# A second Strassen level for one of the seven gate/up block products

## The chip, the cores and the metric

One core of one Trainium2 chip. The metric is the time of one execution on the device, in microseconds (us), as the median of several runs; the run with a profile is one of them, except for the kernel before, whose profiled run (739.01 us) is a separate one. Most runs agree within 0.3%, which is half of what this change can move at most, so the experiments were timed in five rounds against the kernel before on the same chip.

## The reference, cut to what matters

```python
h  = x + attention(layernorm(x))                  # S = 2048 tokens, D = 1024, linear attention, 32 heads
def _B_ref(x, W_gate, W_up, W_down):              # x: (1, 2048, 1024), F = 3584
    gate = jnp.einsum("bsd,df->bsf", x, W_gate)
    up   = jnp.einsum("bsd,df->bsf", x, W_up)
    gate = gate * (gate > 0)
    h = gate * up
    return jnp.einsum("bsf,fd->bsd", h, W_down)
h2 = h + _B_ref(layernorm(h), W_gate, W_up, W_down)
```

All inputs are bf16. The change touches only the two products `gate` and `up`.

Of the kernel before, what the change touches and what calls it, by code (L numbers as in the profile page):

```python
# [8 lines left out]
ALU = mybir.AluOpType  # L9
FP32 = mybir.dt.float32  # L10
BF16 = mybir.dt.bfloat16
# [20 lines left out]
def block_kernel(ctx: ExitStack, tc: tile.TileContext, x, wqkv, wo, wg, wu, wd, out, H: int):  # L32
# [449 lines left out]
    def new_hn(s):  # L482
        aops = mctx.enter_context(tc.tile_pool(name=f"aops{s}", reuse_waits="tile", bufs=1))
        hnT.append([aops.tile([P, KC, SW], BF16, name=f"hn{s}{i}") for i in range(2)])
        hns.append([aops.tile([P, KH, SW], FP16, name=f"hs{s}{k}") for k in range(3)])
# [136 lines left out]
    qctx.close()  # L622


    new_hn(1)
    tpool = mctx.enter_context(tc.tile_pool(name="tpool", reuse_waits="tile", bufs=2))
    mwork = mctx.enter_context(tc.tile_pool(name="mwork", reuse_waits="tile", bufs=2))
# [28 lines left out]
            out.append(ops())  # L656
        return out

    H22, S1, S2, S3, H12, S4, H21 = range(7)

    def wd_sums(c):

        st = {}
        tt = nc.vector.tensor_tensor

        def load():
            raw = fpool.tile([P, 4 * D], BF16, tag="wraw", bufs=2, name="wraw")[:].rearrange("p (k c d) -> p k c d", k=2, c=2)
            for k in range(2):
                nc.sync.dma_start(out=raw[:, k], in_=wd_k[:, k, 2 * c:2 * c + 2, :])
            st["b"] = [[raw[:, k, :, j * DW:(j + 1) * DW] for j in range(2)] for k in range(2)]  # L670

        def one():
            t = fpool.tile([P, 4 * D], BF16, tag="wt", name="wt")
            st["t"] = t[:].bitcast(FP16).rearrange("p (k c d) -> p k c d", k=4, c=2)
            (b11, b12), _ = st["b"]
            tt(out=st["t"][:, 0], in0=b12, in1=b11, op=ALU.subtract)

        def two():
            tt(out=st["t"][:, 1], in0=st["b"][1][1], in1=st["t"][:, 0], op=ALU.subtract)

        def three():
            tt(out=st["t"][:, 2], in0=st["b"][1][1], in1=st["b"][0][1], op=ALU.subtract)

        def four():
            tt(out=st["t"][:, 3], in0=st["b"][1][0], in1=st["t"][:, 1], op=ALU.subtract)
            for k in range(4):
                nc.sync.dma_start(out=t_dram[k][:, 2 * c:2 * c + 2, :], in_=st["t"][:, k])

        return load, [one, two, three, four]

# [15 lines left out]
        nc.sync.dma_start(out=x_dram[s][k][:, H12:S4 + 1, r, :], in_=hq[:, H12:S4 + 1, :])  # L706

    def new_hq():
        return spool[0].tile([P, 7, SW], BF16, tag="hq", bufs=3, name="hq")

    def early_sums(f):

        k, r = divmod(f, FQ)
        st = []

        def load():
            st.append(new_hq())
            nc.sync.dma_start(out=x1[0][k][:, r, :], in_=raw_dram[0][:, f, :])
            for q, j in ((3, H22), (2, H21), (1, H12)):
                nc.sync.dma_start(out=st[0][:, j, :], in_=raw_dram[q][:, f, :])  # L720

        return [load, lambda: None, lambda: None, lambda: hh_sums_a(st[0], 0, f), lambda: hh_sums_b(st[0], 0, f)]
# [3 lines left out]
    def early_quad(s, fc, w):  # L726

        left = left_ops(hnT[s], hns[s])
        gus = {}

        def mm(ps, m, v, start):
            for kc in range(KH):
                nc.tensor.matmul(ps[:], lhsT=w(v, m)[:, kc, :], rhs=left[m - 1][:, kc, :],  # L733
                                 start=(start and kc == 0), stop=(kc == KH - 1), skip_group_check=True)

        def fin(i, j, v, ps, m):
            q = 2 * i + j
            if v == 0:
                gus[q] = mwork.tile([P, 2, SW], BF16, tag="gu", name="gu")
            gu = gus[q]  # L740
            if m is not None:
                nc.vector.tensor_tensor(out=gu[:, v, :], in0=ps[:], in1=m, op=ALU.add)
            if v == 0:
                nc.scalar.activation(out=gu[:, 0, :], in_=ps[:] if m is None else gu[:, 0, :], func=ACT.Relu)
            else:
                d = mwork.tile([P, SW], BF16, tag="hh1", bufs=4, name="hh1")
                nc.vector.tensor_tensor(out=d[:], in0=gu[:, 0, :], in1=ps[:] if m is None else gu[:, 1, :], op=ALU.mult)
                nc.sync.dma_start(out=raw_dram[q][:, fc, :], in_=d[:])

        return strassen(pspool, mwork, mm, fin, 4, False, quad_copies[fc])  # L750
# [39 lines left out]
    for t, copy in ((order[-2], ("m1", 1)), (order[-1], ("u3", 1))):  # L790
        tc.add_manual_dep(squared[t].ins, quad_copies[2][copy].ins.name,
                          mybir.DependencyInfo(mybir.DependencyClass.NoSync, mybir.DependencyReason.DATA),
                          reason="order")
    pqctx.close()
    psctx.close()
    abctx.close()
# [2 lines left out]
    x1pool = ctx.enter_context(tc.tile_pool(name="x1pool", side="right", **reuse))  # L799
    fpool = ctx.enter_context(tc.tile_pool(name="fpool", side="right", **reuse))  # L800
    sctx = ExitStack()
    spool.append(sctx.enter_context(tc.tile_pool(name="spool", side="right", **reuse)))
    ET = mybir.EngineType
    ctx.enter_context(tc.manual_schedule(engines={ET.PE, ET.DVE, ET.Activation}))
# [7 lines left out]
    x1 += new_x(x1pool)  # L812
    add = nc.vector.tensor_tensor

    def quad(s, fc, w, k):

        left = left_ops(hnT[s], hns[s])
        tag = "XY"[k % 2]
        hq = new_hq()
        out = {0: x1[s][fc // FQ][:, fc % FQ, :], 1: hq[:, H12, :], 2: hq[:, H21, :], 3: hq[:, H22, :]}  # L820
        st = {}

        def halves(t):
            return t[:].rearrange("p (v n) -> p v n", v=2)

        def m(n, nm, t=None):
            if t:
# [5 lines left out]
                                     start=(t is not None and kc == 0), stop=(kc == KH - 1), skip_group_check=True)  # L833

        def snap(nm):
            st[nm] = mwork.tile([P, 2, SW], FP32, tag="snap", bufs=4, name="snap")
            nc.scalar.copy(out=st[nm][:], in_=halves(st["A"]))  # L837

        def gu(q, nm, base):
# [5 lines left out]
            add(out=out[q], in0=st[q][:, 0, :], in1=st[q][:, 1, :], op=ALU.mult)  # L845

        def rg():
            st["rg"] = mwork.tile([P, SW], BF16, tag="rg", name="rg")
            nc.scalar.activation(out=st["rg"][:], in_=halves(st["A"])[:, 0, :], func=ACT.Relu)

        def mul2():
# [2 lines left out]

        return {
            "m1": lambda: m(1, "A", "A"), "s1": lambda: snap("m1"), "m2": lambda: m(2, "D", tag),
            "g0": lambda: gu(0, "D", "m1"), "x0": lambda: mul(0), "m6": lambda: m(6, "A"), "s2": lambda: snap("u2"),
            "m5": lambda: m(5, "E", tag), "m7": lambda: m(7, "A"), "s3": lambda: snap("u3"),
            "g3": lambda: gu(3, "E", "u3"), "x3": lambda: mul(3), "m4": lambda: m(4, "A"), "rg": rg, "x2": mul2,
            "m3": lambda: m(3, "E"), "g1": lambda: gu(1, "E", "u2"), "x1": lambda: (mul(1), hh_sums_b(hq, s, fc)),  # L860
        }

    HW = DW // 2
# [59 lines left out]
    for steps, _ in now:  # L923
        for f in steps:
            f()
    prv, k = None, 0
    for r, (wt, f, fi, toks) in enumerate(runs):
        w = [ops() for _, ops in now]
        later = []
        for n, s in enumerate(toks):  # L930
            first = n == 0 and isinstance(wt, int) and fi == 0
            due = (wt + 1 if first else NE // GP if r == GP else 0)
            if r + 1 < len(runs) and n == 0 and not (r == NE - 1):
                now = sums_of_run(r + 1)
                later = [p for steps, _ in now for p in steps]
            take = -(-len(later) // (len(toks) - n))
            work += later[:take]
            del later[:take]
            if r >= NE:
                want = -(-len(fill) // max(nwin - 2 - k, 1))  # L940
                for p in range(want):
                    work.insert(min(len(work), 2 * p + 1), fill.pop(0))
            cur = quad(s, f, w, k)
            cur["m1"]()
            cur["s1"]()
            if prv:
                prv["g3"]()
                slot(0)
                prv["x3"]()
            cur["m2"]()  # L950
            if prv:
                prv["m4"]()
            cur["g0"]()
            slot(1)
            cur["x0"]()
            if prv:
                prv["rg"]()
            cur["m6"]()
            slot(2)
            if prv:  # L960
                prv["x2"]()
            cur["s2"]()
            if prv:
                prv["m3"]()
            if due and due < FH // GP:
                get_group(due)
            slot(3)
            if r == NE - 1:
                now = sums_of_run(r + 1)
                work += [p for steps, _ in now for p in steps]  # L970
            cur["m5"]()
            if prv:
                prv["g1"]()
                slot(4)
                prv["x1"]()
            cur["m7"]()
            cur["s3"]()
            slot(5)
            assert not work
            prv = cur  # L980
            k += 1
# [19 lines left out]
    for n in range(2):  # L1001
        t = fpool.tile([P, 4 * D], BF16, tag="wraw", bufs=2, name="xd")
        fview.append(t[:, 0:FQ * SW].rearrange("p (f t) -> p f t", f=FQ))
    ftile = fpool.tile([P, 4 * D], BF16, tag="wt", name="xd")
    xs_free = [ftile[:, 0:FQ * SW].rearrange("p (f t) -> p f t", f=FQ).bitcast(FP16)]
    for i, t in ((1, fview[0]), (0, fview[1])):
        xtiles[1, i, 0] = t
# [388 lines left out]
```

## The kernel before: what the change and the argument touch

Every large product is done as one level of Strassen in Winograd's form: the operands are cut in 2 x 2 blocks, and seven block products, with sums of blocks as operands, replace eight. In the gate/up stage the tokens and F are halved for the result's blocks, and D for the contraction. A "window" is the work for one tile of 128 columns of F, in both halves of F, and one half of the tokens, for gate and up together. `quad` holds its steps: `m1` to `m7` are the block products on TensorE, `s1` to `s3` copies of a running sum out of PSUM (ScalarE), `g0`, `g1`, `g3` joins of a second PSUM accumulator with such a copy (VectorE), each followed by a ReLU on ScalarE, and `x0` to `x3` the products of gate and up (VectorE).

```python
def quad(s, fc, w, k):
    left = left_ops(hnT[s], hns[s])
    tag = "XY"[k % 2]
    hq = new_hq()
    ...
    def m(n, nm, t=None):                      # one block product: 8 matmuls of 512 columns
        if t:
            st[nm] = acc(t)                    # a new accumulator: [128, 1024] fp32, gate and up
        ps = halves(st[nm])
        for v in range(2):
            for kc in range(KH):               # KH = 4 contraction tiles
                nc.tensor.matmul(ps[:, v, :], lhsT=w[v][n - 1][:, kc, :], rhs=left[n - 1][:, kc, :],
                                 start=(t is not None and kc == 0), stop=(kc == KH - 1), ...)

    def snap(nm):                              # ScalarE: PSUM -> fp32 in SBUF
        st[nm] = mwork.tile([P, 2, SW], FP32, tag="snap", bufs=4, name="snap")
        nc.scalar.copy(out=st[nm][:], in_=halves(st["A"]))

    def gu(q, nm, base):                       # VectorE: join PSUM with a copy; ScalarE: ReLU of the gate half
        g = st[q] = mwork.tile([P, 2, SW], BF16, tag="gu", name="gu")
        add(out=g[:], in0=halves(st[nm]), in1=st[base][:], op=ALU.add)
        nc.scalar.activation(out=g[:, 0, :], in_=g[:, 0, :], func=ACT.Relu)

    def mul(q):
        add(out=out[q], in0=st[q][:, 0, :], in1=st[q][:, 1, :], op=ALU.mult)
    ...
    return {
        "m1": lambda: m(1, "A", "A"), "s1": lambda: snap("m1"), "m2": lambda: m(2, "D", tag),
        "g0": lambda: gu(0, "D", "m1"), "x0": lambda: mul(0), "m6": lambda: m(6, "A"), "s2": lambda: snap("u2"),
        "m5": lambda: m(5, "E", tag), "m7": lambda: m(7, "A"), "s3": lambda: snap("u3"),
        "g3": lambda: gu(3, "E", "u3"), "x3": lambda: mul(3), "m4": lambda: m(4, "A"), "rg": rg, "x2": mul2,
        "m3": lambda: m(3, "E"), "g1": lambda: gu(1, "E", "u2"),
        "x1": lambda: (mul(1), hh_sums_b(hq, s, fc)),   # activation product, one more sum, a store
    }
```

The loop over windows writes the steps of this window and the tail of the previous one (`prv`) in one fixed order. In this stage TensorE, VectorE and ScalarE run exactly the order written. `slot(n)` puts in "filling" pieces of VectorE work: the sums of the next tile's weights, the sums of the down weights, and sums of the activations that an earlier stage stored.

```python
cur["m1"](); cur["s1"]()
prv["g3"](); slot(0); prv["x3"]()
cur["m2"](); prv["m4"]()
cur["g0"](); slot(1); cur["x0"]()
prv["rg"](); cur["m6"](); slot(2); prv["x2"](); cur["s2"]()
prv["m3"](); ...; slot(3)
cur["m5"](); prv["g1"](); slot(4); prv["x1"]()
cur["m7"](); cur["s3"](); slot(5)
```

The sums of the down weights work on 1024 columns at a time, from a load buffer `wraw` into a buffer `wt`, and are stored to DRAM for the down stage.

## Time and profile before

| | value |
|---|---|
| median (3 runs) | 738.68 us (738.03 to 740.35) |
| span of the profiled run | 737.2 us |
| gate/up stage | from 288 to 578 us, 24 windows of 12.09 us |
| TensorE in that stage | 56 matmuls a window, 0.2159 us start to start, no idle time |
| VectorE in that stage | 222 us busy, 77% |

The profile page's fourth part follows the chain of work that ended last back from the end, and gives its shares by engine. Of the kernel before:

```profile
PE 85%; DVE 7%; DMA 4%; ACT 3%; issue 1%; SPq 0%; DVEq 0%; POOL 0%; ACTq 0%
```

TensorE (PE) carries it. VectorE (DVE) has slack. In the list of waits of VectorE in the gate/up stage (columns: engine, what waited, what it waited for; us in total, times, longest) the top line is

```profile
DVE tg L640 <- PE accA L832: 21.9, 11, 2.0
```

The first weight sum for the next tile waits for a buffer of weight sums that TensorE is still reading: 11 times, about 2.0 us each. This is idle time of an engine off the path. It costs nothing here, but it shows that VectorE's 77% can't all be moved about at will.

### The profile page before, as it was taken

The numbers are of one execution on the slowest core, as the hardware profiler recorded it, in microseconds if no ns is written. First come the engines' busy times: TensorE is split into PE (matmuls) and PEld (weight loads), VectorE is DVE, ScalarE is ACT, GpSimd is POOL, SyncE is SP. The second block draws the span as 40 slices with busy tenths as digits, with TensorE's granted clock in tenths as the row PEclk, the third lists the DMA queues.
The fourth block names the chain that finished last, engine by engine and source line by source line (L and its number), as shares of the span: only waits on it lengthen the run. The fifth ranks groups of instructions, "written<-read, shape, count | busy, mean of one in ns | idle before, by whom it ended". The sixth has DMA issues, their size and how long they took to land.

```text
span 737.2 us, 10549 instructions
## 1 busy us (share of the span) xinstructions
PE 722.7 (98%) x3967; PEld 381.8 (52%) x4020; DVE 556.0 (75%) x980; ACT 321.5 (44%) x580; POOL 20.7 (3%) x56
## 2 busy tenths in 40 slices
PE   8999999999989999999999999999999999999997
PEld 3444555444444444444444444444444458888667
DVE  6997644676789767688768787887786479996677
ACT  4776553778786655444344444443444120000000
POOL 0000000000000000000000000000000001100210
PEclk9999999999999999999999999999999999999999
DMA  9765002079977526175638358575483499978932
GB/s 315 169 145 157 0 1 95 21 168 230 215 166 166 135 73 208 43 207 135 196 106 243 114 188 270 182 219 193 162 280 120 137 392 343 305 253 283 257 44 58
DMA packets 143811, 128.88 MB, mean 175 GB/s; under 512 B 50960, under 2 KB 126096, under 8 KB 143760
## 3 DMA queue, kind: packets, MB, share of 16 engines
q1 hardware_dynamic: 136688, 123.30, 55.6%
q0 software_dynamic: 5312, 3.15, 3.4%
q10 hardware_dynamic: 1760, 1.77, 0.7%
q8 instruction: 31, 0.51, 0.3%
q14 instruction: 20, 0.16, 0.1%
HBM read 76.81 MB, written 39.85 MB: 158 GB/s over the span
## 4 chain that ended last, share of the span: by engine, by line
PE 85%; DVE 7%; DMA 4%; ACT 3%; issue 1%; SPq 0%; DVEq 0%; POOL 0%; ACTq 0%
PE accA L832 22%; PE accX L832 8%; PE accY L832 8%; PE accA L1167 8%; PE attn L557 6%; PE Aq L733 4%; PE Aq L314 3%; PE accA L993 3%; PE accX L1167 3%; PE Aq L454 3%; PE accY L1167 2%; PE Eq L314 2%; PE accY L993 2%; PE accX L993 2%; PE Eq L733 2%; DVE stats L272 1%
## 5 line engine op out<-in xcount | busy, mean ns | idle before, releaser
L842 ACT ACTIVATE gu<-gu 128x512 bf16<-128x512 bf16 x72 | 45.4, 630 | 131.3 <-DVE gu L841 131.3
L837 ACT COPY snap<-accA 128x1024 f32<-128x1024 f32 x72 | 72.5, 1008 | 36.5 <-PE accA L832 36.4
L832 PEld LDWEIGHTS <-tg 128*128 128x128 f16 x384 | 37.6, 98 | 45.3
L832 PEld LDWEIGHTS <-tu 128*128 128x128 f16 x384 | 37.6, 98 | 45.3
L557 PE MATMUL attn<-wo_mem,oT 128*128 128x512 bf16 x247 | 57.9, 379 | 2.6 <-DVE o_sb L534 1.3
L841 DVE TENSOR_TENSOR gu<-accY,snap 128x1024 bf16<-128x1024 f32 x36 | 43.9, 1219 | 10.0 <-ACT snap L837 10.0
L832 PE MATMUL accA<-hn,tg 128*128 128x512 f16 (+1 forms) x192 | 49.3, 379 | 0.0
L832 PE MATMUL accA<-hn,tu 128*128 128x512 f16 (+1 forms) x192 | 49.3, 379 | 0.0
L841 DVE TENSOR_TENSOR gu<-accX,snap 128x1024 bf16<-128x1024 f32 x36 | 43.9, 1219 | 6.4 <-PE accX L832 3.7
L154 ACT COPY u<-Aq 128x512 f32<-128x512 f32 x54 | 31.3, 581 | 36.6 <-PE Aq L314 19.3
L1167 PEld LDWEIGHTS <-x 128*128 128x128 f16 (+1 forms) x448 | 43.9, 98 | 5.5
L832 PEld LDWEIGHTS <-wu 128*128 128x128 bf16 x288 | 28.2, 98 | 34.0
L832 PEld LDWEIGHTS <-wg 128*128 128x128 bf16 x288 | 28.2, 98 | 34.0
L557 PEld LDWEIGHTS <-oT 128*128 128x128 bf16 x256 | 24.6, 98 | 32.5 <-issue 4.1
L845 DVE TENSOR_TENSOR hq<-gu 128x512 bf16<-128x512 bf16 x48 | 20.3, 423 | 14.3 <-ACT gu L842 14.2
L314 PEld LDWEIGHTS <-xT 128*128 128x128 bf16 (+1 forms) x192 | 18.6, 98 | 23.6 <-issue 2.3
L534 DVE TENSOR_TENSOR o_sb<-nd,rd 128x384 bf16<-128x384 f32 (+1 forms) x48 | 23.4, 508 | 8.3 <-ACT rd L533 6.1
L1131 POOL DMA_DIRECT2D out_dram<-o x12 | 15.2, 1265 | 508.8 <-DMA h<-h_dram 419.1
L1167 PEld LDWEIGHTS <-xs 128*128 128x128 f16 x280 | 27.4, 98 | 3.2
L560 DVE SCALAR_TENSOR_TENSOR x_res<-attn,x_res 128x512 bf16<-128x512 f32 x32 | 22.0, 686 | 8.6 <-PE attn L557 8.5
L1173 DVE TENSOR_TENSOR snap<-accA,u 128x1024 f32<-128x1024 f32 x16 | 19.5, 1221 | 11.4 <-PE accA L1167 11.3
L993 PEld LDWEIGHTS <-x 128*128 128x128 bf16 (+1 forms) x168 | 16.4, 98 | 19.6
(235 smaller groups left out, 1420.3 us busy)
## 6 DMA issues: line engine op xcount, KB each, us to landing
x<-x_dram SPq DMA_DIRECT2D x17, 896.0 KB, 8.8
x_dram<-hq SPq DMA_DIRECT2D x28, 512.0 KB, 3.2
wg<-in_B_W_gate_dram SPq DMA_DIRECT2D x14, 512.0 KB, 5.1
wu<-in_B_W_up_dram SPq DMA_DIRECT2D x14, 512.0 KB, 7.3
wraw<-in_B_W_down_dram SPq DMA_DIRECT2D x14, 512.0 KB, 4.9
x_dram<-hq SPq DMA_DIRECT2D x28, 256.0 KB, 2.7
t_dram<-wt SPq DMA_DIRECT2D x28, 256.0 KB, 2.2
xd<-x_dram SPq DMA_DIRECT2D x6, 896.0 KB, 6.9
```

The costliest lines, as they stand in the source:

```text
L154: copies[nm, v] = nc.scalar.copy(out=snaps[nm, v], in_=bank[v][:])
L314: nc.tensor.matmul(ps[:], lhsT=left[m - 1][:, kc, r + v * P:r + (v + 1) * P], rhs=right[m - 1][:, kc, :], start=(start and kc == 0), stop= ...
L454: nc.tensor.matmul(ps[:], lhsT=rq[m - 1][:, kc, (c + v) * P:(c + v + 1) * P], rhs=left[m - 1][:, kc, :], start=(start and kc == 0), stop=( ...
L534: nc.vector.tensor_tensor(out=ov[:, c0:c0 + n], in0=ndv[:, :, 0:P].rearrange("p k (h e) -> p k h e", h=HPC), in1=rd[:, 0:n, :].unsqueeze(3 ...
L557: nc.tensor.matmul(ps[:], lhsT=st["oT"][:, c, :], rhs=wo_sb[:, c, j * NW:(j + 1) * NW], start=(c == 0), stop=(c == KC - 1))
L733: nc.tensor.matmul(ps[:], lhsT=w(v, m)[:, kc, :], rhs=left[m - 1][:, kc, :], start=(start and kc == 0), stop=(kc == KH - 1), skip_group_ch ...
L832: nc.tensor.matmul(ps[:, v, :], lhsT=w[v][n - 1][:, kc, :], rhs=left[n - 1][:, kc, :], start=(t is not None and kc == 0), stop=(kc == KH - ...
L837: nc.scalar.copy(out=st[nm][:], in_=halves(st["A"]))
L841: add(out=g[:], in0=halves(st[nm]), in1=st[base][:], op=ALU.add)
L842: nc.scalar.activation(out=g[:, 0, :], in_=g[:, 0, :], func=ACT.Relu)
L993: nc.tensor.matmul(ps[:, t * NW:(t + 1) * NW], lhsT=x_tile(n, s, kh)[:, f, (t0 + t) * P:(t0 + t + 1) * P], rhs=w_tile(n, kh)[:, f, :], sta ...
L1167: nc.tensor.matmul(pv[:, tt, :], lhsT=left(m)[:, f, tt * P:(tt + 1) * P], rhs=right(m)[:, f, :], start=(t is not None and f == 0 and tt % ...
```

## The change

Intent: save matmuls. In the last 20 windows (5 groups of two F tiles by two token halves), the second product `m2` of the four windows of a group is itself a 2 x 2 problem: two F tiles by two token halves. It is done with a second Strassen level, called the cross: 7 products of 4 matmuls in place of 4 products of 8. The four results stay in SBUF in fp32 (`res`), and each window's `g0` joins accumulator A with its stored result, where it joined the accumulator of `m2` with a copy of A.

```diff
-    def quad(s, fc, w, k):
+    def quad(s, fc, w, first=None):
         left = left_ops(hnT[s], hns[s])
-        tag = "XY"[k % 2]
+        tag = new_tag()
         hq = new_hq()
-        st = {}
+        st = {"r": first}
...
-            "g0": lambda: gu(0, "D", "m1"),
+            "g0": lambda: gu(0, "A", "r") if first is not None else gu(0, "D", "m1"),
...
+    def cross(wt, res):
+        ...
+        def mm(n, nm, t=None):
+            ...
+            for v in range(2):
+                for kc in range(KQ):                       # KQ = 2: half the contraction
+                    nc.tensor.matmul(ps[:, v, :], lhsT=right(v, n)[:, kc, :], rhs=cross_left(n)[:, kc, :], ...)
+        def snap(q):
+            nc.scalar.copy(out=res[q][:], in_=halves(st["A"]))
+        def join(q, nm):
+            add(out=res[q][:], in0=halves(st[nm]), in1=res[q][:], op=ALU.add)
...
+            if grouped and fi == GP - 1 and wt + 1 < FH // GP:   # weight sums for the next group's cross
+                c = cross_weight_sums(wt + 1)
+                work += c[4 * n:4 * n + 4]
...
+            if first:                                       # first window of a group
+                x = cross(wt, res)
+                x["p1"](); x["c1"](); prv["g3"]()
+                x["p2"](); x["j00"](); prv["m4"](); slot(0); prv["x3"]()
+                prv["m3"](); prv["rg"](); prv["x2"]()
+                x["p6"](); x["c2"](); x["p5"]()
+                prv["g1"]()
+                slot(1)
+                prv["x1"]()
+                cur = quad(s, f, w, res[s, fi])
+                cur["m1"]()
+                x["p7"](); x["c3"]()
+                slot(2)
+                cur["g0"]()
+                cur["m5"](); ...; x["j11"](); slot(3)
+                cur["m6"](); cur["s2"](); cur["x0"]()
+                x["p4"](); x["c4"](); slot(4); x["p3"](); x["j01"]()
+                cur["m7"](); cur["s3"](); slot(5)
+            elif grouped:                                   # the other three windows: as before, without m2
+                ...
```

(Calls put on common lines here; cuts marked.) To find room in SBUF, the activation block `hq` goes from 3 buffers of 7 parts to 2 of 6, the buffer `wt` gets smaller, and the third down-weight sum is made in place in the load buffer.

In the kernel before, `g0` had its result from `m2` and a copy of A, so `m6`, which adds to A, had to wait only for that copy (`s1`, ScalarE). Now `g0`, on VectorE, reads A itself, after `m1`, and `m6` must wait for `g0`.

Names in the prediction: the "sixth product" is `m6`, and likewise for the others, "old" ones being those of `prv`; the "block 11 join" is `g0`, the "block 12 join" is `g1` and the "block 22 join" is `g3`. In the cross, `p1` to `p7` are the products, `c1` to `c4` the copies, and `j00`, `j11`, `j01` the joins.

## The prediction

> **What bounds the kernel now.** I read the page's busy line, then a table of stretches over the gate/up stage, then the list of waits, then the timeline of two windows.
>
> ```profile
> PE 722.7 (98%) x3967; PEld 381.8 (52%) x4020; DVE 556.0 (75%) x980; ACT 321.5 (44%) x580; POOL 20.7 (3%) x56
> ```
>
> TensorE is busy 98% of the span and weight loads 52%, so loads hide behind matmuls and TensorE's instruction count sets the time, unless something makes it wait. The gate/up stage that the change touches runs from 288 to 578 us. It is 24 windows (one F tile, one token half) of 7 block products, each product 8 matmuls (gate and up, 4 contraction tiles). Stretches of one window each (columns: us, busy us and instructions of each engine, granted clock, DMA share, GB/s):
>
> ```profile
> 457.32:469.41 12.09, 12.04 (x56) 5.49 (x56) 10.51 (x20) 5.20 (x7) 0.00 (x0) 1.00 0.38 136
> 541.95:554.04 12.09, 12.04 (x56) 5.48 (x56) 11.40 (x21) 5.09 (x7) 0.00 (x0) 1.00 0.86 281
> sum 290.16, PE 288.85 PEld 131.52 DVE 222.21 ACT 125.02 POOL 0.00; mean PE 12.04 PEld 5.48 DVE 9.26 ACT 5.21 POOL 0.00
> ```
>
> Every window takes 12.09 us: 56 matmuls at 0.2159 us. VectorE averages 9.26 of 12.09 us, ScalarE 5.21. The clock is 1.00, so no throttle is in play. The list of waits, cut to TensorE and to 290-560 us, is empty; the groups say the same in their last column (idle before):
>
> ```profile
> L832 PE MATMUL accA<-hn,tg 128*128 128x512 f16 (+1 forms) x192 | 49.3, 379 | 0.0
> L832 PE MATMUL accA<-hn,tu 128*128 128x512 f16 (+1 forms) x192 | 49.3, 379 | 0.0
> ```
>
> So here a matmul removed is 0.216 us gained, and any new wait of TensorE is lost in full. The other engines matter only through such waits. Their durations, from the timeline of one window:
>
> ```profile
> 367.49 0.42 DVE L645 TENSOR_TENSOR tg<-wg 128x512 f16<-128x512 bf16 x1
> 367.82 1.22 DVE L841 TENSOR_TENSOR gu<-accY,snap 128x1024 bf16<-128x1024 f32 x1
> ...
> 368.95 0.42 DVE L704 TENSOR_TENSOR hq<-hq 128x512 f16<-128x512 bf16 x1
> ...
> 370.80 1.03 PE L832 MATMUL accY<-hn,wg 128*128 128x512 bf16 x4
> 370.93 1.22 DVE L841 TENSOR_TENSOR gu<-accX,snap 128x1024 bf16<-128x1024 f32 x1
> 371.00 1.01 ACT L837 COPY snap<-accA 128x1024 f32<-128x1024 f32 x1 [0.34 <-PE accA L832]
> ```
>
> Back to back, VectorE instructions start about 0.08 us before the one ahead has ended: 367.82 to 368.95 is 1.13 us for a 1.22 us join. And a ScalarE copy starts 0.20 us after TensorE has moved on from the bank pair (370.80 to 371.00).
>
> **What the Trainium skill says.**
> - "TensorE: Matmul & The Clock Gate", section "Wait — 56ns, not 53.3ns?": back-to-back matmuls of N=512 start 215.7 ns apart at the full clock. The trace agrees: 12.09 us / 56 = 215.9 ns.
> - "VectorE: DVE Perf Modes", section "What auto-detection actually checks": a two-source operation of 16-bit data can run two elements a cycle, and `tensor_tensor` gets no further. In the trace 512 bf16 columns take 0.42 us and 1024 take 0.68, 0.52 ns a column; the 1024-column join of PSUM with an fp32 tile takes 1.22.
> - "PSUM — Partial Sum Buffer", section "Specifications (TRN2)": 8 banks of 512 fp32 a partition. An accumulator here is 1024 columns, so two "A", one "X" and one "Y" fill all 8 banks. The change can get no fifth; the cross product must borrow these four.
> - The same page, section "Engine vs sequencer instructions": ScalarE and VectorE queues are strict FIFO. So a late join holds everything after it, which is what could go wrong here.
>
> **The change part by part.** There are 5 groups of two F tiles by two token halves, the last 20 windows. Each window's second product (A12·B21) is taken away: 4 x 8 = 32 matmuls a group. Instead a 2x2 Strassen over the pair of F tiles and the two halves makes the four results in 7 products of 4 matmuls (contraction halved to 2 tiles): 28. TensorE's order confirms it: 8002 rows against 8042, 20 weight loads and 20 matmuls fewer. Gain: 20 x 0.2159 = 4.32 us. The instruction orders of all engines agree up to the gate/up stage, so nothing is gained or lost before it.
>
> ScalarE, per group: four copies of the first product go, four of the cross products come. No change (5.21 of 12.09 us leaves room).
>
> VectorE, per group: the four gate/up joins with the first product stay (their other input is now the stored cross result); 3 joins in fp32 come, 3 x 1.14 = 3.4 us; 8 weight sums of 256 columns come, which no row shows, estimated from 0.42 and 0.68 us for 512 and 1024 as 0.29 us, or 0.22 start to start: 1.8 us. Once, 4 left sums of 1024 columns: 4 x 0.6 = 2.4. Altogether 5 x 5.2 + 2.4, near 28 us more. Against start-to-start costs of 1.14 (join), 0.70 (PSUM product), 0.36-0.38 (512 bf16) and 0.60 (1024 bf16), the order of before sums to 222.5 us, the measured 222.2; that of after to about 251 in 285.8 us: 88%, from 77%.
>
> The stage stays TensorE's on average, but not in each window, because the time is shared out unevenly. A regular window is now 6 products, 48 x 0.2159 = 10.36 us; a first window of a group is 6 products and the cross, 76 x 0.2159 = 16.41. VectorE's load, counted from its order:
> - a quad without extras: 3 joins, 3 products, one PSUM product, 4 sums: 6.76 us;
> - first window: 6.76 + 3 joins 3.42 + 4 weight sums 1.44 + 2 or 3 pieces of down-weight sums at 0.60: 12.8 to 13.4 of 16.41;
> - the window after it: 8.2 to 10.0 of 10.36;
> - the two windows of the second tile: 6.76 + 1.44 + 4 cross sums 0.88 + pieces: 10.3 with two pieces, 10.9 with three.
> Carried forward, VectorE's backlog never passes 0.75 us (the third group's entry, where 0.2 and 0.5 add up), and each first window empties it.
>
> How much backlog does TensorE tolerate? Time 0 is the end of the last product of the previous window. The copy of that bank ends at 0.20 + 1.01 = 1.21.
> - Regular window: first product 0-1.73; old fourth product 1.73-3.45 (needs that copy, margin 0.5); old third 3.45-5.18 (needs the join of block 22 read by 1.25 + 1.22 = 2.5, margin 0.9); sixth 5.18 (needs the block 11 join, ended at 3.7, margin 1.5). The next copy must not be held by the ReLU in front of it in ScalarE's queue: the join of block 12 ends at 9.2 to 10.4, its ReLU 0.65 later, the copy is wanted at 10.56, and has the 0.5 of margin on top. With three pieces this is the tightest place.
> - First window: the new first product needs its accumulator back at 6.9, when VectorE has done join 22, fp32 join, two sums, two products: about 5.6 to 6.3, margin 0.6. The sixth is wanted at 11.2 and its join ends by 10.5.
> So backlogs up to half a microsecond cost nothing, and in one to three entries of a group some 0.1-0.2 us may be lost: I put 0.3 us in all. Sum: 738.68 - 4.32 + 0.3 = 734.7.
>
> **Rivals.**
> 1. VectorE becomes the bound. For: 88% on average, 10.9 of 10.36 us in the windows with three pieces, joins in strict order with ScalarE in between, accumulators with one product less of time between them (before, the first and second product lay between the copy and the fourth product, 3.45 us; now 1.73). Against: the first window absorbs 3 us, and before, VectorE spent 22 us waiting for the weight-sum buffer that it now need not wait for. If every one of the 20 windows lost 0.2 us, the gain would be gone: 738.4. If half lost 0.2, 736.4.
> 2. Stores hold VectorE up: the block of activations has two buffers in place of three, and the third down-weight sum is now stored from its load buffer. For: a store takes 2.2 to 3.2 us to land, and the sync engine's queue has waits up to 15 us. Against: between a quad's last store and the second next quad's first write lie about 15 us, those long waits are for data not yet made, and a load has some 20 us to come. If it hit each group once with 1 us: 739.
> 3. The gain is not seen at all, since another chain ends last. Against: the chain through this stage is TensorE alone. 738.7.
> 4. Large failure, a transfer late for each group's weights (released later, read at the second tile's first window): 5 x 3 us would give 750. The weights are asked for about 18 us ahead and land in 5 to 7, so I give this little.
>
> **Range and chances.** The gain is capped at 4.32 us, 0.6%; so below 734.4 only the spread of runs (738.03 to 740.35) helps. Rivals 1 and 2 in part reach 737. I take 734.7, with 733.6 to 737.2 for 8 in 10. A 2% gain would need 14.8 us, three times what there is: 0.005. A loss of 2% needs 0.95 us of wait in each of 20 windows less the gain: 0.01. Within 2%: 0.985.
>
> **What would show it.** Right: 20 matmuls fewer; gate/up windows of 10.4 and 16.4 us; TensorE without idle time there; VectorE about 250 us busy over the stage, copies and ReLUs as before in number; the down stage unchanged and 4 us earlier. Wrong: idle time of TensorE before its fourth or third product on the copy or the join (rival 1), VectorE's activation products or down-weight sums waiting for a store (rival 2), a cross weight sum waiting for a load (rival 4), or a longer down stage, which I have taken as unchanged.

## The result, and the profile after

| | before | after |
|---|---|---|
| median | 738.75 us (738.03 to 740.35) | 737.44 us (736.51 to 738.55) |
| runs | 4 | 4 |
| profiled run | 739.01 us (span 737.2) | 736.51 us (span 734.7) |

The ratio after/before is 0.998, with a 95% interval of 0.9957 to 1.0003. A ratio here is the mean time of one kernel's fast runs over the mean of the other's fast runs of the same rounds, so it is not quite the ratio of the medians. The class is "the same" (within 2%). The median of 737.44 lies 2.7 us above the predicted 734.7, and just outside the range.

The profiled run of the changed kernel is its fastest one, so its trace tells a slightly rosy story; its stage also began 0.7 us earlier than that of before (287.20 against 287.92), which is scatter of the stage ahead, where both kernels issue the same instructions in the same order (a variant of the kernel before that differs only inside the stage, tried below, began it at 286.99).

The page of the changed kernel, busy line:

```profile
PE 719.6 (98%) x3947; PEld 380.0 (52%) x4000; DVE 580.4 (79%) x1039; ACT 325.0 (44%) x580; POOL 20.8 (3%) x56
```

20 matmuls and 20 weight loads have gone, ScalarE has as many instructions as before, and VectorE is busy 24 us longer. The table of stretches, with two regular windows and two first windows of a group:

```profile
444.92:455.28 10.36, 10.36 (x49) 4.70 (x48) 8.65 (x16) 4.41 (x6) 0.00 (x0) 1.00 0.79 222
465.64:476.01 10.37, 10.32 (x48) 4.70 (x48) 10.06 (x21) 4.39 (x7) 0.00 (x0) 1.00 0.45 159
476.01:492.56 16.55, 16.45 (x75) 7.44 (x76) 14.55 (x26) 8.49 (x11) 0.00 (x0) 1.00 0.91 261
523.64:540.77 17.13, 16.47 (x76) 7.42 (x77) 15.04 (x28) 8.82 (x11) 0.00 (x0) 1.00 0.75 243
```

The regular windows take the predicted 10.36 us. A first window has 76 matmuls and should take 76 x 0.2159 = 16.41; these two take 16.55 and 17.13. The list of waits of TensorE, cut to the stage, was empty before and has one line now:

```profile
PE accA L851 <- DVE gu L860: 1.8, 4, 0.8
```

L860 is the join in `gu`, L851 the matmul in `m`. The five places in the timeline (columns: start in us, duration, engine, line, operation, output<-inputs; in brackets the idle time before it and what ended it):

```profile
344.31 1.02 PE L851 MATMUL accA<-hs,tg 128*128 128x512 f16 x4 [0.83 <-DVE gu L860]
...
392.12 1.02 PE L851 MATMUL accA<-hs,tg 128*128 128x512 f16 x4 [0.17 <-DVE gu L860]
...
439.98 1.02 PE L851 MATMUL accA<-hs,tg 128*128 128x512 f16 x4 [0.22 <-DVE gu L860]
...
487.60 1.02 PE L851 MATMUL accA<-hs,tg 128*128 128x512 f16 x4
...
535.80 1.02 PE L851 MATMUL accA<-hs,tg 128*128 128x512 f16 x4 [0.56 <-DVE gu L860]
```

All five are `m6` of a group's first window. The bracket understates the loss: a matmul's recorded duration (0.379 us) overlaps the next one's start (0.216 us later), so a stall of up to 0.163 us leaves no idle time at all in this view. From start to start, less the regular 0.216, the losses are 0.99, 0.33, 0.38, 0.14 and 0.72 us: **2.56 us in all**. There is no other loss in the stage. So the net gain in these traces is 4.32 - 2.56 = 1.76 us; with the 0.72 us by which this run's stage began earlier it makes 2.5, the difference of the two spans.

The timeline of the third group's first window shows the wait from VectorE's side. Time 0 of the prediction is the start of the cross's first product, 428.38. `m6` is wanted 52 matmuls later, at 428.38 + 52 x 0.2159 = 439.61.

```profile
428.38 0.59 PE L939 MATMUL accA<-hn,wg 128*128 128x512 bf16 x2
...
435.93 1.22 DVE L860 TENSOR_TENSOR gu<-accY,snap 128x1024 bf16<-128x1024 f32 x1
...
437.07 0.42 DVE L646 TENSOR_TENSOR tg<-wg,tg 128x512 f16<-128x512 bf16 x1
437.25 0.63 ACT L861 ACTIVATE gu<-gu 128x512 bf16<-128x512 bf16 x1 [1.61 <-DVE gu L860]
...
437.91 0.43 DVE L864 TENSOR_TENSOR hq<-gu 128x512 bf16<-128x512 bf16 x1 [0.42 <-ACT gu L861]
438.37 0.42 DVE L708 TENSOR_TENSOR hq<-hq 128x512 f16<-128x512 bf16 x1
438.71 1.22 DVE L860 TENSOR_TENSOR gu<-accA,snap 128x1024 bf16<-128x1024 f32 x1
```

The first join (435.93, `prv`'s `g1`) is followed by a weight sum (`slot(1)`). Then comes the activation product of `prv` (L864), which stands still 0.42 us for its ReLU on ScalarE, then its sum (L708), and only then the join `g0` that TensorE needs. It ends at 439.93, and `m6` starts at 439.98, 0.37 us late. Between the two joins lie three instructions and an idle wait, and TensorE needs none of them soon.

In all five first windows, counted in the same way (us after the start of the cross's first product; `m6` is wanted at about 11.22 in each):

| group | `g1` starts | `g0` starts | `g0` ends | `m6` starts | instructions between |
|---|---|---|---|---|---|
| 1 | 6.69 | 10.94 | 12.16 | 12.21 | 7 |
| 2 | 7.17 | 10.28 | 11.50 | 11.55 | 4 |
| 3 | 7.55 | 10.33 | 11.55 | 11.60 | 3 |
| 4 | 6.71 | 10.09 | 11.31 | 11.36 | 4 |
| 5 | 7.29 | 10.67 | 11.89 | 11.94 | 4 |

Two things vary: how late `g1` starts, and how much lies between `g1` and `g0`, which is the order written. A late `g1` is in groups 3 and 5 the backlog that VectorE brings in. In group 2 it is not: VectorE came in early and stood idle before `prv`'s `g3`, and three filling sums of `slot(0)`, ahead of `g1`, made it late. In group 1 `slot(2)` holds four sums, a weight sum and three of stored activations, where group 2 has one; the weight sums held back from the window before fill its slots.

The chain that ended last has changed with it:

```profile
PE 67%; DVE 18%; ACT 7%; DMA 5%; issue 2%; SPq 0%; DVEq 0%; ACTq 0%; POOL 0%
```

VectorE's share rose from 7% to 18%, some 80 us, for 2.56 us of loss. At a wait this view goes over to the engine waited for and follows that engine's work back. The share says that the chain went over, not how much it cost there.

### The profile page after: what moved, and what is told of

The parts are those of the page before. It is cut to its first block, busy times and chain, and to the rows that moved or that the text cites. A ratio compares the mean times of both kernels' runs of the same rounds, so it can differ in the third digit from the quotient of the medians.

```text
span 734.7 us, 10578 instructions
## 1 busy us (share of the span) xinstructions
PE 719.6 (98%) x3947; PEld 380.0 (52%) x4000; DVE 580.4 (79%) x1039; ACT 325.0 (44%) x580; POOL 20.8 (3%) x56
## 4 chain that ended last, share of the span: by engine, by line
PE 67%; DVE 18%; ACT 7%; DMA 5%; issue 2%; SPq 0%; DVEq 0%; ACTq 0%; POOL 0%
PE accA L851 15%; PE accA L1345 8%; PE attn L557 5%; PE accX L851 4%; PE Aq L314 3%; DVE gu L860 3%; PE accA L1171 3%; PE accY L851 3%; PE Aq L738 3%; PE accX L1345 3%; PE Aq L454 3%; PE accY L1345 2%; PE Eq L314 2%; PE accY L1171 2%; PE accX L1171 2%
## 5 line engine op out<-in xcount | busy, mean ns | idle before, releaser
L856 ACT COPY snap<-accA 128x1024 f32<-128x1024 f32 x52 | 52.5, 1012 | 65.2 <-PE accA L851 65.0
L851 PEld LDWEIGHTS <-tg 128*128 128x128 f16 x384 | 37.5, 98 | 47.9 <-issue 3.2
L851 PEld LDWEIGHTS <-tu 128*128 128x128 f16 x384 | 37.6, 98 | 45.3
L851 PE MATMUL accA<-hn,tg 128*128 128x512 f16 (+1 forms) x192 | 49.3, 379 | 0.0
L851 PE MATMUL accA<-hn,tu 128*128 128x512 f16 (+1 forms) x192 | 49.3, 379 | 0.0
L860 DVE TENSOR_TENSOR gu<-accX,snap 128x1024 bf16<-128x1024 f32 x26 | 31.7, 1221 | 10.6 <-ACT snap L856 8.3
L860 DVE TENSOR_TENSOR gu<-accY,snap 128x1024 bf16<-128x1024 f32 x26 | 31.7, 1220 | 7.5 <-ACT snap L856 7.5
L851 PEld LDWEIGHTS <-wu 128*128 128x128 bf16 x208 | 20.4, 98 | 24.5
L851 PEld LDWEIGHTS <-wg 128*128 128x128 bf16 x208 | 20.4, 98 | 24.5
L864 DVE TENSOR_TENSOR hq<-gu 128x512 bf16<-128x512 bf16 x48 | 20.3, 423 | 10.3 <-ACT gu L861 10.3
```

## The experiments

There were two theories.

- **Theory A, order.** VectorE has enough time in each first window, but `g0` stands too far back in its queue, behind work that nothing needs yet. Moved forward it costs nothing, and the full 4.3 us come out.
- **Theory B, amount.** VectorE's extra 25 us are too much for the first windows. Moving `g0` forward only moves the wait to another place.

All eight kernels were reported as giving a correct result. Two of them are wrong and are named as such; the tolerance of the comparison doesn't notice either, so "correct" proves little for such small omissions. Kernels of one job shared their runs of the kernel before: 738.86 us in the first job (737.88 to 739.71, 11 runs), 738.47 in the second (737.91 to 739.0, 9 runs).

### The changed kernel again

No edit. The first medians differ by 1.31 us (738.75 - 737.44) on four runs each, with an interval that includes no gain at all, where the traces give 1.76. So I first asked whether the gain is there and whether the waits come back in the same places.

> The changed kernel once more, unchanged, for a narrower interval. From its profile TensorE loses 2.6 us start to start in the gate/up stage, always before the sixth product of a group's first window (0.99, 0.33, 0.38, 0.14, 0.72 us), so 4.3 - 2.6 = 1.7 us faster than before: ratio about 0.9977. If instead the stall is peculiar to the profiled run, the losses will differ in size or place and the ratio may be 0.994 or 1.000.

Measured: 736.67 us (736.1 to 736.98), ratio 0.9971 (0.9959 to 0.9983). The losses before `m6` are 0.98, 0.33, 0.37, 0.12 and 0.71 us, the same places and sizes to 0.03 us. The waits follow from the program, not from chance. 738.86 x (1 - 0.9971) = 2.1 us of gain with an interval of about 1.3 to 3.0 holds the 1.76 of the traces; the first job's medians, 1.3 us apart with few runs, lie on the other side of 1.76.

### The join ahead of the previous window's product

```diff
                 slot(1)
-                prv["x1"]()
                 cur = quad(s, f, w, res[s, fi])
                 cur["m1"]()
                 x["p7"]()
                 x["c3"]()
-                slot(2)
                 cur["g0"]()
+                prv["x1"]()
+                slot(2)
                 cur["m5"]()
```

> The changed kernel with one reordering: in a group's first window the block 11 join is put directly behind the block 12 join, before the block 12 product, its dependent sum and the filling pieces. Theory A (the sixth product waits for a join that stands too late in VectorE's order): the five waits go to zero, the stage takes 2.6 us less, ratio to before about 0.9942. Theory B (VectorE is short of time over the group as a whole): the waits move to another product of the same or the next window and the time stays within 0.5 us of the changed kernel's.

Measured: **734.31 us** (733.89 to 736.32), ratio 0.9947 (0.9934 to 0.9959). In this kernel's trace, the list of waits of TensorE in the stage is empty. The table of stretches has TensorE busy for every part of a stretch that begins just ahead of the stage and ends a little into the next:

```profile
286.90:576.00 289.10, 289.10 (x1341) 130.85 (x1340) 247.26 (x469) 127.27 (x168) 0.00 (x0) 1.00 0.57 180
```

VectorE does practically the same work as in the changed kernel (467 instructions and 246.75 us there, in the same stretch). Its timeline in the third group's first window, for comparison with the one above:

```profile
434.56 1.22 DVE L860 TENSOR_TENSOR gu<-accY,snap 128x1024 bf16<-128x1024 f32 x1
...
435.70 0.42 DVE L646 TENSOR_TENSOR tg<-wg,tg 128x512 f16<-128x512 bf16 x1
...
436.03 1.22 DVE L860 TENSOR_TENSOR gu<-accA,snap 128x1024 bf16<-128x1024 f32 x1
...
437.16 0.42 DVE L864 TENSOR_TENSOR hq<-gu 128x512 bf16<-128x512 bf16 x1
...
438.24 1.03 PE L851 MATMUL accA<-hs,tg 128*128 128x512 f16 x4
```

`g0` now starts 1.47 us after `g1`, where it was 2.78. The activation product behind it (437.16) no longer waits for its ReLU, which ran during the join: the 0.42 us of idle time has gone too. In all five groups `g0` ends between 10.06 and 10.26, about a microsecond before `m6` is wanted. Nor could it come much sooner: in groups 1 and 2 VectorE stood idle before it (0.59 and 0.11 us) until `m1` was done. Theory A holds, and B in its plain form is refuted. The chain that ended last is TensorE's again:

```profile
PE 84%; DVE 7%; ACT 4%; DMA 4%; issue 1%; SPq 0%; DVEq 0%; POOL 0%; ACTq 0%
```

### The cross's weight sums made only once

Wrong: groups 2 to 5 use the cross weight sums of group 1. This takes eight VectorE instructions out of the two windows ahead of each of those first windows, and leaves the order alone. It asks how much of the loss is the backlog that comes in from there.

```diff
-            if grouped and fi == GP - 1 and wt + 1 < FH // GP:
+            if False and grouped and fi == GP - 1 and wt + 1 < FH // GP:
```

> Wrong results on purpose: the 8 weight sums of the cross product are made for the first group only, which takes 4 x 0.2 us out of each of the two windows before groups 2 to 5. If the backlog brought in by them is what makes the join late, the waits of groups 2 to 5 (0.33, 0.38, 0.14, 0.72) fall to about zero, 0 to 0.2 us each, and the first group's 0.99 stays: about 1.3 us faster than the changed kernel, ratio to before about 0.996. If the order within the first window alone is to blame, all five stay.

Measured: 735.82 us (735.27 to 736.11), ratio 0.9959 (0.9947 to 0.9971). The losses are 0.98, 0.33, 0, 0.07 and 0.07, together 1.45 in place of 2.56.

```profile
PE accA L851 <- DVE gu L860: 1.0, 2, 0.8
```

Groups 3 to 5 lose almost nothing now. Group 2 keeps all of its 0.33, against the expectation: it had no backlog to lose (`prv`'s `g3` starts at 1.24 here and 1.25 there, after idle time in both), and with four instructions and the ReLU wait between `g1` and `g0`, and filling sums ahead of `g1`, the order alone is enough there. So of the 2.56 us, 1.11 come from the order together with a backlog that these sums bring in, and 1.45 from the order without it. The forward move cures both, since `g0` then ends a microsecond early.

### The kernel before, less twenty matmuls

Wrong: in one window in four of the last 20, `m2` uses half of its contraction for gate and up, which takes 20 matmuls out and changes nothing else.

```diff
-                for kc in range(KH):
+                for kc in range(KH // 2 if n == 2 and k >= NE and k % 4 == 0 else KH):
```

> Wrong results on purpose: the kernel before, with 4 matmuls of the second product left out in the first window of each of the five groups, 20 in all, and nothing else. If a matmul in this stage is worth its pitch of 0.2159 us, it is 4.3 us faster: ratio 0.9942. If less comes out (2 us or under), the first step of the prediction's sum fails, not the wait.

Measured: 734.05 us (733.75 to 735.07), ratio 0.9939 (0.9927 to 0.9951). That is 738.86 x 0.0061 = 4.5 us for 20 matmuls; the pitch of 0.2159 us gives 4.32, well within the interval. The price of a matmul in the prediction is right, and the kernel with the join moved forward (0.9947) reaches it: the cross's extra 25 us of VectorE work can lie wholly beside TensorE.

### All filling pieces behind the join

Two kinds of work stood between `g1` and `g0`: the product of `x1` with its wait for the ReLU, and filling pieces. Here `x1` stays in front, straight after `g1`, and only the filling pieces of two slots go behind `g0`.

```diff
                 prv["g1"]()
-                slot(1)
                 prv["x1"]()
                 ...
-                slot(2)
                 cur["g0"]()
+                slot(1)
+                slot(2)
                 cur["m5"]()
```

> The changed kernel, but in a group's first window only the filling pieces between the block 12 join and the block 11 join go behind the latter; the block 12 product, which waits for its ReLU on ScalarE, and its dependent sum stay in front. If the filling pieces are the larger part of the order's share, the waits before the sixth product fall from 0.99, 0.33, 0.38, 0.14, 0.72 to about 0, 0, 0.4, 0, 0.1: 2 us faster than the changed kernel, ratio 0.995. If the ReLU's round trip is the larger part, over 1.5 us of the 2.56 stays.

Measured: 736.12 us (735.98 to 738.41), ratio 0.9978 (0.9966 to 0.9991). The loss before `m6` came out as expected (0, 0, 0.37, 0, 0.10), so with `x1` still in front 0.47 of the 2.56 us stay, and the filling pieces were the larger part. The time didn't come out as expected. A new wait of TensorE, 1.95 us start to start, stands in the window after the last group's first one. The waits of TensorE in this kernel:

```profile
PE accY L851 <- DVE gu L860: 1.8, 1, 1.8
PE accA L851 <- DVE gu L860: 0.2, 1, 0.2
```

Its timeline shows where the 1.8 comes from:

```profile
532.59 0.42 SPq L977 DMA_DIRECT2D wd<-in_B_W_down_dram  x1
...
534.21 0.33 SPq L691 DMA_DIRECT2D t_dram<-wt  x1
...
540.53 0.69 DVE L680 TENSOR_TENSOR wt<-wraw 128x1024 f16<-128x1024 bf16 x1 [4.55 <-DMA xd<-x_dram]
...
543.88 1.02 PE L851 MATMUL accY<-hs,wg 128*128 128x512 f16 x4 [1.78 <-DVE gu L860]
```

VectorE stood 4.55 us before the first sum of a new down-weight piece (L680). That sum writes `wt`, which has one buffer, and the stores of the piece before (L691) had to have left it. The view names another transfer (L986, issued at 534.63), but that one took 7.8 us and landed after the sum had begun; the store is what this instruction depends on. The DMA list, cut to this store, gives its size and the us from issue to landing:

```profile
t_dram<-wt SPq DMA_DIRECT2D x1, 256.0 KB, 6.1
```

So it landed at 540.31, 0.22 us before the sum. It was issued at 534.21, after a load of 896 KB of down weights at 532.59. In the changed kernel the store of the same piece went out at 534.64, ahead of that load at 535.07, took 2.7 us, and the sum ran at 537.46 without a wait. The kernel with the join moved forward has the wait too. There the load (529.84) is also ahead of the store (533.47), the store took 4.5 us, and VectorE stood 2.95 us, which did not reach TensorE. Its list of waits of VectorE has the line

```profile
DVE wt L680 <- DMA t_dram<-wt: 3.7, 2, 3.0
```

The kernel before shows the same order and 2.57 us of idle VectorE. That the load in front delays the store is argued from these orders and was not tried. What is shown is that the prediction's second rival exists: a store can hold VectorE and, in this kernel, through it TensorE; the changed kernel has its store ahead of the load and does not wait. The buffer is `wt`, though, which had no second one in the kernel before either, and not one of the two that the prediction named.

### How much room there is: the join once, twice, three times

The best order, with the join `g0` of the five first windows repeated (the same operands, the same result). Each repetition is one join of VectorE work just ahead of the deadline. If the deadline that I read out of the trace, 11.22, is the right one, there is 1.0 us to spare, and beyond that each microsecond of VectorE costs a microsecond of the kernel, five times over.

```diff
-            add(out=g[:], in0=halves(st[nm]), in1=st[base][:], op=ALU.add)
+            for again in range(2 if base == "r" and fc % GP == 0 and s == 0 else 1):   # 3 in the third kernel
+                add(out=g[:], in0=halves(st[nm]), in1=st[base][:], op=ALU.add)
```

Once (the best order without an edit, run again):

> The reordered kernel again, unchanged, for a second interval and as the reference of the next two runs: no wait of TensorE in the gate/up stage, ratio 0.994 to 0.9955.

Measured: 734.3 us (733.79 to 735.06), ratio 0.9946 (0.9933 to 0.9958), no loss in the stage.

Twice:

> The reordered kernel with the block 11 join of each group's first window made twice (same inputs, same output), 1.13 us more of VectorE five times. The join ended 0.9 to 1.1 us before the sixth product wanted it. If that margin is what counts, the second join all but fits: waits of 0 to 0.25 us in each group, 0.5 us in all, not the 5.7 us that were added. If VectorE's total is the bound, about 5 us are lost.

Measured: 735.69 us (735.45 to 736.73), ratio 0.9966 (0.9952 to 0.998). The losses at `m6` are 0.15, 0.15, 0.31, 0.15 and 0.15, 0.90 in all. On top came 0.80 us that I hadn't expected: in group 1 the cross's third product `p3` waited for the join `j11` behind the repeated `g0`. And 0.05 us were lost in the window after the last group's first one, where VectorE had stood 2.20 us for the store of down-weight sums.

Three times:

> The same with the join made three times, 2.27 us more five times. The margin is used up by the first, so the third costs its full 1.13 us in each group: 6.2 us of waits in all before the sixth products, about 740.5 us, ratio 1.0025. If later waits hide part of it, 3 to 5 us.

Measured: 742.42 us (741.7 to 744.1), ratio 1.0056 (1.0043 to 1.0069). The losses at `m6` are 1.41, 1.41, 1.57, 1.41 and 1.41, and 0.81 at `p3` in group 1; 8.0 in all. The waits of TensorE in this kernel:

```profile
PE accA L851 <- DVE gu L861: 6.4, 5, 1.4
PE accX L940 <- DVE cr L947: 0.6, 1, 0.6
```

The kernel is 8.1 us slower than the one with a single join, as the losses say.

The first repetition adds 1.26 us to each window (joins that write the same tile start 1.26 us apart, where independent ones start 1.14 apart) and costs 0.15; the second adds 1.26 more and costs 1.26 more (1.41 - 0.15). So the room is there and is as large as the trace said: about 1.1 us of VectorE work are free, the rest is paid in full. What I missed, at 0.8 us, is that `g0` is not the only deadline: in group 1, where four sums of `slot(2)` stand behind `g0`, that of the next join, `j11`, is as near.

## Why the prediction was wrong, point by point

**Right**: the class; the price of the 20 matmuls, 4.32 us, which two experiments show; the load of ScalarE, which didn't change (only its ReLU ahead of one product mattered, as part of the wait below); the regular windows of 10.36 us; VectorE's load, predicted as about 251 us and measured as 246 to 247; the small weight sums, estimated as 0.29 us and measured as 0.28; no wait for a late load (rival 4) and none for a store in this kernel (rival 2). From the first matmul of the down stage to the end of the span both traces take 162.7 us, so the down stage is unchanged. VectorE's wait for the weight-sum buffer, which the prediction counted as time set free, shrank from 21.9 to 2.8 us:

```profile
DVE tg L642 <- PE accA L851: 2.8, 2, 2.0
```

**The step that failed** is in the paragraph on how much backlog TensorE tolerates: "The sixth is wanted at 11.2 and its join ends by 10.5." The 11.2 was right to 0.02 us; the 10.5 was not. The prediction doesn't show how it is made up, but it can't be laid to the backlog alone: the margin of 0.7 us was set against a backlog of up to 0.75. With the backlog of the cross's sums taken away ("made only once") the join of groups 3 to 5 still ends at 10.65, 11.24 and 11.24, so in two of three the margin was gone before any backlog came in. What stands ahead of the join and used the margin up: the filling pieces of the slots (four sums in the first group's `slot(2)`), and the wait of the product for its ReLU (0.42 us in the third group). In the changed kernel's trace, with the backlog, the join ends at 11.31 to 12.16. That a first window has 3 us of VectorE time to spare was true of the window as a whole and didn't help, since the deadline comes at 11.2 of its 16.4 us. The strict queue of VectorE, cited from the Trainium skill in the prediction ("PSUM — Partial Sum Buffer", section "Engine vs sequencer instructions"), agrees with these traces: the join that TensorE waited for stood behind a product that waited 0.42 us for its ReLU. So the term "0.3 us in all" of the sum was mis-sized: it measured 2.56. With it the sum is 738.7 - 4.3 + 2.6 = 737.0, between the two medians that the changed kernel showed (737.44 and 736.67).

**The wrong place was called tight.** The prediction gave its smallest margin, 0.5 us, to the regular windows' fourth product, and called the copy behind it the tightest place. The regular windows never waited, not once in 15 windows, even where VectorE had 10.06 us of work in 10.37. The other check in the first window, that the accumulator is back by 6.9, held: in the third group the product that frees it (434.08, 0.69 us long) ended 6.39 us after the window's start.

**The rivals.** Rival 1, VectorE as the bound, was right in its sign, and its two cases (losses of 2.0 and 4.0 us) enclose the 2.56 measured. That is luck: its mechanism was wrong, since 15 of the 20 windows lost nothing and five lost 0.14 to 0.99, and the amount of VectorE's work is not the bound, as the moved join shows. Rival 2 lies in wait: one step in the order away, it cost 1.95 us.

**What stays open.** The two jobs put the changed kernel at 0.998 and 0.9971 with overlapping intervals; why the first one's four runs spread over 2 us isn't known. Why the store lands late (6.1 and 4.5 us where the load is in front, 2.7 where it isn't) is argued only.

The version with the join ahead of the previous window's product is the best: 734.31 and 734.3 us in two jobs, about 4 us below the kernel before and 2.4 below the changed kernel of the same job (736.67 - 734.31). It is not free of rival 2: VectorE stands 2.95 us for a store in it, so far without TensorE waiting.

## What to carry to other kernels

An engine busy less than 90% of the time can still be late five times out of five: for each instruction that another engine waits for, write down when it is wanted and everything that stands ahead of it in its queue, with the backlog that comes in and the waits of those in front, and not only its window's own work. Then order the queue by who needs what first: moving one 1.2 us join ahead of a product, its sum and a slot of filling pieces that nobody needed yet was worth 2.4 us, more than the whole second Strassen level had brought until then. Work saved on the bound engine also moves its own deadlines forward, so expect the saving to be eaten first where a result is handed back to it.

## What the Trainium skill lacked or had wrong

- "TensorE: Matmul & The Clock Gate", section "Back-to-back issue gap", gives about 131 ns for each matmul of N=512 in a sustained stream of weight loads and matmuls, and calls 216 ns the gap of an isolated one. Here some 1,340 such pairs (24 windows of 56 in the kernel before) follow one another in the stage at 215.9 ns (56 in 12.09 us, 48 in 10.36), without idle time. That agrees with the 215.7 ns of the section cited in the prediction, and not with the 131.
- "VectorE: DVE Perf Modes", section "The DRAIN you can't avoid", says that the next operation doesn't start until the pipeline has emptied, and that one that is not held starts earlier, without saying by how much. Here independent joins of 1.22 us start 1.14 us apart (0.08 us before the recorded end of the one ahead), joins that write the same tile 1.26 us apart, and a sum that reads the product just ahead of it (0.43 us long) starts after 0.46 us.
- I found no page with the price of a handover between VectorE and TensorE through an accumulator in PSUM. Here `m6` starts 0.05 us after the recorded end of the join (11.55 to 11.60 in the third group).
